# Routing's small operations moved ahead of a step's shares, masks behind them, and the low weight product last, in window attention followed by a top-1 mixture of experts

## Chip, cores and metric

The kernel runs on one core of one Trainium2 chip. The metric is the device time in microseconds (us) of one launch, the median of several runs.

## What is computed

Attention in a causal window of 64 positions (8 batches, 8 heads, 576 positions, 64 values a head), and behind it a mixture of 8 experts in which each of the 4608 tokens (rows of 512 values) goes to one expert only. The reference, cut:

```python
scores = scale * np.matmul(q, k.transpose(0, 1, 3, 2))
mask = (rel >= 0) & (rel < window)                 # window = 64
attn = softmax(np.where(mask, scores, -1e9))       # 1e-9 is added to the sum
x = np.matmul(attn, v)                             # to 4608 rows of 512
logits = x @ w_gate                                # 8 experts
expert_idx = np.argmax(logits, axis=1)
gate_w = softmax(logits)[np.arange(N), expert_idx]
for e in range(8):
    mask = expert_idx == e
    h = np.maximum(x[mask] @ w1[e], 0.0)           # 512 -> 1024
    out[mask] = gate_w[mask, None] * (h @ w2[e])   # 1024 -> 512
```

## The kernel before

All is written in the order in which each engine runs it; nothing reorders it later. Attention runs in 36 **steps** of 128 tokens (`NS`), counted by `i` in the loop at L797, and 7 more empty ones (`LAST`). It is a pipeline over steps: in step `i` the kernel makes the scores of tile `i`, the exponentials of tile `i-1`, the masks of `i-2`, the values and shares of `i-3`, the transposed rows of `i-4`. What one step issues on each engine:

- ScalarE (ACT): `exps(i-1)`, eight Exp of 64 columns; `evac(i-2)`, the copy `tsb` of the transposed exponentials out of PSUM tile `t_b`; `cols_t(i-4)`, the copy `xT`; a piece of weight rounding `whi`.
- GpSimd (POOL): `apart(i-2)`, two multiplications `pm` of `tsb` with masks, 512 columns each. These are the **masks**.
- VectorE (DVE): `folded(i)` and `largest(i)` on the scores in `s_b` (L386, L392, L394); `shares(i-3)` (L438, L440, L442), which reads `x_b`, divides, and writes the row `xrow`; then a read of the logits, `lgT` (L495) in one step and `lgs` (L479) in the next; a piece of the weights' low part `wlo` (L228).
- TensorE (PE): `scores(i)` into `s_b`, `values(i-3)` into `x_b`, a product for the logits (also in `x_b`), `rows_t(i-4)` (L449), `transp(i-1)` (L407). Within `x_b` the next writer waits for the last reader, so `values` of a step waits for the `lgT` or `lgs` of the step before.

**Routing** runs in three rounds, of 14, 12 and 10 tiles. When the logits of a round's last tile have been read, `route` queues eight pieces, s1 to s8, in `slow`. s1 to s3 find each token's expert (`lm`, `ld`, `eq`, `em`, `oh` on DVE). s4 is PE's: it counts ranks (L528, L530), ACT copies them (`rks`), at the head of a step. s5 to s7 turn ranks into places (`pos`, `base`, `se`, `pf`, `g` on DVE; `se`, `fl`, `mid` on POOL). s8 splits them (`lo`, `val`), and then one-hot rows `hot_row` (`put`, L577) and their products `here`, `said` (L588 to L595) follow from the queue `puts`. From these PE makes a table (L602), DVE reads it (L607 to L615), and POOL fetches token rows by index (L172). Round 0 is routed in steps 19 to 26, round 1 in steps 31 to 37, so that experts 0 to 3 can begin on their first tokens while attention still runs.

From step 29 (`TURN`) on, `forward` lays pieces of the first experts' work (the generator `expert`) between a step's parts, and `turn` transposes fetched rows: PE into `t_b` or `m_b`, ACT `xeh`, DVE `xel`. From step 29 on `s_b` has one buffer for scores, and `rows_t` shares `t_b` with `turn`.

Each f32 product of the experts is made of three matmuls of rounded parts: high by high, high weights by low tokens, low weights by high tokens. An expert pass has 8 groups `j`; each has a first product of 12 matmuls into `m_b` or `t_b` (L293), then `hh` (ACT) and `hl` (DVE), and a second product of three matmuls for each of 2 or 3 blocks (L257). `yield` in `expert` marks where `forward` may cut. ACT's `whi` and DVE's `wlo` for group `j+1` are made while group `j` runs.

Of the kernel before, what the change touches and what calls it, by code (L numbers as in the profile page):

```python
# [24 lines left out]
P = 128  # L25
# [15 lines left out]
NS = N // P  # L41


ROUNDS = [14, 12, 10]
# [18 lines left out]
RATE = (3, 2)  # L63
# [51 lines left out]
def window_attention_then_top1_moe(ctx: ExitStack, tc: tile.TileContext, qkv, wall, wg, cst, out):  # L115
    nc = tc.nc
# [157 lines left out]
    def expert(xt, idx, gates, wts, following=None):  # L274


        xh, xl = xt
        nu = len(idx)
        w = nu * P
        yp = None  # L280
        cur = wts.first
        for j in range(NJ):
            if j + 1 < NJ:
                nxt = wts.split()
            elif following is not None:
                following().first = following().split()
            hi, lo = cur
            hp = bank("hp")
            m = 0
            for kk in range(4):  # L290
                ks = slice(kk * P, (kk + 1) * P)
                for a, x in ((hi, xh), (hi, xl), (lo, xh)):
                    nc.tensor.matmul(hp[:, 0:w], lhsT=a[:, ks], rhs=x[:, kk, 0:w], start=(m == 0), stop=(m == 11))  # L293
                    m += 1
                if kk < 3:
                    yield
            hh = hw.tile([P, WIDE * P], F32R, name="hh")
            hl = hw.tile([P, WIDE * P], F32R, name="hl")
            nc.scalar.activation(out=hh[:, 0:w], in_=hp[:, 0:w], func=AF.Relu)  # L299
            nc.vector.scalar_tensor_tensor(out=hl[:, 0:w], in0=hp[:, 0:w], scalar=0.0, in1=hh[:, 0:w],  # L300
                                           op0=ALU.max, op1=ALU.subtract)
            yield
            yield from flush()
            if yp is None:
                yp = [bank("yp") for u in range(nu)]
            late.append(((hh, hl), yp, cur, j, (idx, gates) if j == NJ - 1 else None))
            cur = nxt
            yield j
# [45 lines left out]
    def begin_routing():  # L354
        nc.vector.tensor_copy(out=tri, in_=cc("tri"))
        nc.vector.tensor_copy(out=base, in_=cc("ebase"))
        nc.vector.tensor_copy(out=val[:, :, 0], in_=cc("tcol"))
        nc.vector.tensor_copy(out=rowb, in_=cc("row"))
# [128 lines left out]
    slow, puts, begin = deque(), deque(), deque()  # L487
# [9 lines left out]
    def route(nt, lgs, t0, rnd):  # L497
# [80 lines left out]
                                    in1=v["lo"][:, a:b].unsqueeze(2).to_broadcast([P, b - a, P]), op=ALU.is_equal)  # L578


        again = (None,) if rnd + 1 < len(ROUNDS) else ()
        slow.extend((f in (None, s4), f) for f in (s1, s2, s3, *again, s4, s5, s6, s7, s8))

    def parts(pool, want, nt, nm):

# [177 lines left out]
    def each(f, n):  # L763
        if 0 <= n < NS:
            f(n)
# [4 lines left out]
    def first_passes():  # L770
        for e in range(EARLY):
            ms = range(2 * e, 2 * e + 2)
            for j in expert(xe[e % 2], cols(eidx, ms), cols(egate, ms), ew[e],
# [6 lines left out]
                        keep["turned"] = True  # L780
                yield e, j

    early = first_passes()

    def forward(i, place):
# [10 lines left out]
    with tc.manual_schedule():  # L796
        for i in range(NS + LAST):  # L797
# [10 lines left out]

            rs_["step"] = i
            if slow and slow[0][0]:  # L810
                f = slow.popleft()[1]
                if f:
                    f()
            while begin and begin[0][0] <= i:
                begin.popleft()[1]()
            each(exps, i - 1)
            each(evac, i - 2)
            each(apart, i - 2)
            while exs:
                exs.popleft()()  # L820
            if i > TURN:
# [4 lines left out]
            each(largest, i)  # L826
            if i == 3:
                begin_routing()
            if TURN - 2 <= i < TURN:
                turn(xg[0], i - TURN + 2, xe[0], m_b)  # L830
            forward(i, 1)
# [4 lines left out]
            if quarters:  # L836
                o, w = quarters.popleft()
# [9 lines left out]
            if rs_["read"]:  # L847
                rs_["read"]()
                rs_["read"] = None
            for k in range(RATE[0] if i < NS else 4):  # L850
                if slow and not slow[0][0]:
                    slow.popleft()[1]()
            for k in range(RATE[1] if i < NS else 4):
                if puts and not slow:
                    puts.popleft()()
            while lows:
                lows.popleft()()
            if pieces:
# [95 lines left out]
```

## Time and profile before

| what | value |
|---|---|
| three runs | 670.57, 672.99, 674.42 us; median 672.99 |
| the profiled execution | 670.88 us, of which its span 669.1 us |
| busy share of the span | PE 93%, DVE 62%, ACT 54%, POOL 29% |
| mean granted PE clock | 0.989 of full speed |
| chain that ended last | PE 73%, DVE 11%, issue 6%, ACT 3%, POOL 3%, DMA 2% |

The profile is of one execution. An instruction's time runs from its start to its end, and what stands in brackets behind a row is how long its engine had been idle and what it waited for. PE's rows overlap, since matmuls are pipelined: starts are read, not ends. Attention alone runs until about 133 us, attention beside the first experts until about 205, and the experts from there on.

### The profile page before, as it was taken

How to read it: one execution, taken by the hardware profiler on the slowest of the kernel's cores; microseconds unless marked ns; L12 is line 12 of the kernel's file. 1: busy time of each engine (PE TensorE's matmuls, PEld its weight loads, DVE VectorE, ACT ScalarE, POOL GpSimd, SP SyncE). 2: the span in 40 equal slices, each digit the busy share in tenths (PEclk: the TensorE clock that was granted, in tenths of full speed). 3: DMA queues.
4: the chain of work that ended last, by engine and by line, in shares of the span. 5: the costliest groups of instructions: out<-in, count | busy, mean ns of one | idle time of the engine just before them, and what ended most of it. 6: DMA issues, size and time to landing. Idle time of an engine off the chain costs nothing.

```text
span 669.1 us, 17037 instructions
## 1 busy us (share of the span) xinstructions
PE 619.5 (93%) x7001; PEld 546.9 (82%) x7001; DVE 413.4 (62%) x762; ACT 359.8 (54%) x758; POOL 193.0 (29%) x168
## 2 busy tenths in 40 slices
PE   6799976888998799999999999999999999999995
PEld 5688865666787688889999999999999999899994
DVE  3777789856775985654444565565556565555651
ACT  4576665555544344454545555655555565555551
POOL 4566654733543015121111131312212131110011
PEclk9999997899999999999999999999999999999998
DMA  9988887864037346664455676576667656555620
GB/s 318 325 282 271 276 291 219 247 212 158 35 132 278 128 157 221 259 225 152 145 171 173 229 225 207 198 233 232 208 225 229 223 195 230 209 203 189 220 95 33
DMA packets 35110, 138.13 MB, mean 206 GB/s; under 512 B 4940, under 2 KB 6092, under 8 KB 25552
## 3 DMA queue, kind: packets, MB, share of 16 engines
q1 hardware_dynamic: 28624, 118.08, 52.3%
q0 software_dynamic: 6400, 18.88, 8.3%
q8 instruction: 57, 0.93, 0.6%
q14 instruction: 29, 0.24, 0.1%
HBM read 119.11 MB, written 19.92 MB: 208 GB/s over the span
## 4 chain that ended last, share of the span: by engine, by line
PE 73%; DVE 11%; issue 6%; ACT 3%; POOL 3%; DMA 2%; POOLq 0%; DVEq 0%; ACTq 0%
PE m_b L293 16%; PE x_b L257 14%; PE s_b L257 14%; PE t_b L293 13%; PE x_b L432 5%; PE s_b L375 3%; POOL pm L418 3%; PE s_b L183 2%; DVE wlo L228 2%; ACT pf L402 2%; PE t_b L407 1%; PE x_b L494 1%; DMA raw<-wall 1%; PE m_b L449 1%; DVE s_b L392 1%
## 5 line engine op out<-in xcount | busy, mean ns | idle before, releaser
L228 DVE TENSOR_TENSOR wlo<-raw,whi 128x1024 fp32r<-128x1024 f32 (+1 forms) x158 | 188.0, 1191 | 165.3 <-ACT whi L231 164.4
L231 ACT CAST whi<-raw 128x1024 fp32r<-128x1024 f32 (+1 forms) x147 | 148.9, 1014 | 100.3 <-PE s_b L257 50.7
L418 POOL TENSOR_TENSOR pm<-tsb,cs 128x512 f32<-128x512 f32 x72 | 91.8, 1295 | 85.2 <-ACT tsb L411 75.2
L265 POOL DMA_INDIRECT out<-ys,idx_sb x32 | 40.7, 1273 | 181.6 <-ACT ys L264 176.7
L172 POOL DMA_INDIRECT xg<-xs,idx_sb x32 | 33.4, 1043 | 155.8 <-PE s_b L183 138.4
L402 ACT ACTIVATE pf<-s_b,mxs 128x64 f32<-128x64 f32 x288 | 63.1, 337 | 14.9 <-PE s_b L375 6.7
L293 PE MATMUL t_b<-xh,whi 128*128 128x256 f32 (+1 forms) x240 | 70.3, 293 | 0.0
L293 PE MATMUL m_b<-xh,whi 128*128 128x256 f32 (+1 forms) x240 | 70.3, 293 | 0.0
L257 PE MATMUL s_b<-whi,hh 128*128 128x512 f32 x176 | 70.0, 398 | 0.0
L293 PE MATMUL m_b<-xl,whi 128*128 128x256 f32 (+1 forms) x240 | 69.6, 290 | 0.2 <-DVE xl L186 0.2
L257 PE MATMUL s_b<-whi,hl 128*128 128x512 f32 x176 | 69.0, 392 | 0.6 <-DVE hl L300 0.6
L293 PE MATMUL t_b<-xl,whi 128*128 128x256 f32 (+1 forms) x240 | 69.4, 289 | 0.0
L293 PE MATMUL m_b<-xh,wlo 128*128 128x256 f32 (+1 forms) x240 | 69.3, 289 | 0.0
L293 PE MATMUL t_b<-xh,wlo 128*128 128x256 f32 (+1 forms) x240 | 69.2, 289 | 0.0
L257 PE MATMUL s_b<-wlo,hh 128*128 128x512 f32 x176 | 69.1, 393 | 0.0
L299 ACT ACTIVATE hh<-m_b 128x256 fp32r<-128x256 f32 (+1 forms) x82 | 32.6, 398 | 58.1 <-PE m_b L293 58.0
L432 PE MATMUL x_b<-ring,pm 64*64 64x65 f32 x2176 | 46.8, 226 | 13.4 <-DVE lgs L479 4.2
L432 PEld LDWEIGHTS x_b<-ring,pm 64*64 64x64 f32 x2176 | 41.5, 138 | 18.9 <-issue 12.6
L257 PE MATMUL x_b<-wlo,hh 128*128 128x512 f32 x144 | 56.5, 392 | 0.0
L257 PE MATMUL x_b<-whi,hl 128*128 128x512 f32 x144 | 56.4, 392 | 0.0
L257 PE MATMUL x_b<-whi,hh 128*128 128x512 f32 x144 | 56.3, 391 | 0.0
L300 DVE SCALAR_TENSOR_TENSOR hl<-m_b,hh 128x256 fp32r<-128x256 f32 (+1 forms) x82 | 35.4, 431 | 22.1 <-ACT hh L299 22.0
(178 smaller groups left out, 1275.6 us busy)
## 6 DMA issues: line engine op xcount, KB each, us to landing
raw<-wall SPq DMA_DIRECT2D x74, 1024.0 KB, 5.2
ring<-qkv SPq DMA_DIRECT2D x66, 386.0 KB, 4.4
xs<-xrow SPq DMA_DIRECT2D x36, 256.0 KB, 3.2
raw<-wall SPq DMA_DIRECT2D x8, 256.0 KB, 5.0
ring<-qkv SPq DMA_DIRECT2D x4, 256.0 KB, 4.8
ring<-qkv SPq DMA_DIRECT2D x4, 130.0 KB, 4.9
ring<-qkv SPq DMA_DIRECT2D x1, 512.0 KB
xg<-xs,idx_sb POOLq DMA_INDIRECT x32, 4.1
```

What stands on the lines that cost most here:

```text
L172: nc.gpsimd.indirect_dma_start(out=t[:, u], out_offset=None, in_=xs[0:rows], in_offset=bass.IndirectOffsetOnAxis(ap=ix, axis=0), bounds_ch ...
L228: nc.vector.tensor_tensor(out=lo[:, s], in0=raw[:, s], in1=hi[:, s], op=ALU.subtract)
L231: nc.scalar.copy(out=hi[:, s], in_=raw[:, s])
L257: nc.tensor.matmul(y, lhsT=x[:, us], rhs=w[:, C:], start=(j == 0 and m == 0), stop=(j == NJ - 1 and m == 2))
L265: ins = nc.gpsimd.indirect_dma_start(out=out, out_offset=bass.IndirectOffsetOnAxis(ap=ix, axis=0), in_=ys, in_offset=None, bounds_check=N ...
L293: nc.tensor.matmul(hp[:, 0:w], lhsT=a[:, ks], rhs=x[:, kk, 0:w], start=(m == 0), stop=(m == 11))
L299: nc.scalar.activation(out=hh[:, 0:w], in_=hp[:, 0:w], func=AF.Relu)
L300: nc.vector.scalar_tensor_tensor(out=hl[:, 0:w], in0=hp[:, 0:w], scalar=0.0, in1=hh[:, 0:w], op0=ALU.max, op1=ALU.subtract)
L375: nc.tensor.matmul(sp[cols, a, g], lhsT=q_r[rows, r, g], rhs=k_r[rows, r - 1:r + 1, g], start=True, stop=True)
L402: nc.scalar.activation(out=pf[:, g, a], in_=sp[:, a, g, 0], func=AF.Exp, bias=mx[:, h:h + 1], scale=SCALE)
L418: nc.gpsimd.tensor_tensor(out=pm[i], in0=t.rearrange("p (g q) -> p g q", g=NG), op=ALU.mult, in1=cc("mask")[:, i * P:(i + 1) * P].unsqueez ...
L432: nc.tensor.matmul(x_b[cols, a, g * V1:(g + 1) * V1], lhsT=pm[i][rows, g, cols], rhs=v_r[rows, c % RING - i, g], start=(i == 0), stop=(i = ...
```

## The change

1. Pieces of routing were run at a step's end, behind `shares` and the read. Now the function `routing` runs them right behind `largest(i)`, ahead of `turn`, `values` and `shares`, for steps below 36.
2. `apart` (the masks on POOL) was called at a step's head; now it is called behind `routing`.
3. Rounds 0 and 1 had an empty entry ahead of s4, which held it back by one step; it is gone. Since s1 to s3 now run a step later than before, s4 to s8 and the `puts` stay in the steps in which they were.
4. The first expert product runs its eight matmuls of the high weights first and its four of the low weights last, cut by `yield` after 4, 8 and 10 matmuls (before: after 3, 6 and 9, the low part third in each group of three).

```diff
             hp = bank("hp")
-            m = 0
             for kk in range(4):
                 ks = slice(kk * P, (kk + 1) * P)
-                for a, x in ((hi, xh), (hi, xl), (lo, xh)):
-                    nc.tensor.matmul(hp[:, 0:w], lhsT=a[:, ks], rhs=x[:, kk, 0:w], start=(m == 0), stop=(m == 11))
-                    m += 1
-                if kk < 3:
+                for x in (xh, xl):
+                    nc.tensor.matmul(hp[:, 0:w], lhsT=hi[:, ks], rhs=x[:, kk, 0:w], start=(kk == 0 and x is xh), stop=False)
+                if kk & 1:
+                    yield
+            for kk in range(4):
+                nc.tensor.matmul(hp[:, 0:w], lhsT=lo[:, kk * P:(kk + 1) * P], rhs=xh[:, kk, 0:w], start=False,
+                                 stop=(kk == 3))
+                if kk == 1:
                     yield
...
-        again = (None,) if rnd + 1 < len(ROUNDS) else ()
-        slow.extend((f in (None, s4), f) for f in (s1, s2, s3, *again, s4, s5, s6, s7, s8))
+        slow.extend((f is s4, f) for f in (s1, s2, s3, s4, s5, s6, s7, s8))
...
+    def routing(a, b):
+        for k in range(a):
+            if slow and not slow[0][0]:
+                slow.popleft()[1]()
+        for k in range(b):
+            if puts and not slow:
+                puts.popleft()()
...
             each(evac, i - 2)
-            each(apart, i - 2)
...
             each(largest, i)
             if i == 3:
                 begin_routing()
+            if i < NS:
+                routing(*RATE)
+            each(apart, i - 2)
...
-            for k in range(RATE[0] if i < NS else 4):
-                if slow and not slow[0][0]:
-                    slow.popleft()[1]()
-            for k in range(RATE[1] if i < NS else 4):
-                if puts and not slow:
-                    puts.popleft()()
+            if i >= NS:
+                routing(4, 4)
```

On DVE, from the read at the end of step 19 into step 20 (round 0; `lm` to `oh` are s1 to s3; the three rows on `s_b_75` are `folded` and `largest` of step 20), before:

```order
L479 TENSOR_REDUCE lgs<-x_b 128x16
L508 TENSOR_REDUCE lm<-lgs 128x14
L511 TENSOR_TENSOR ld<-lgs,lm 128x112
L513 SCALAR_TENSOR_TENSOR eq<-ld,cs_82 128x112
L520 TENSOR_REDUCE em<-eq 128x14
L522 MEMSET oh 128x4
L523 TENSOR_TENSOR oh<-eq,em 128x112
L386 COPY_PREDICATED s_b_75<-fold,s_b_75 128x8x64
L392 TENSOR_REDUCE s_b_75<-s_b_75 128x8
L394 TENSOR_SCALAR mxs<-s_b_75 128x8
L438 TENSOR_SCALAR den<-x_b 128x8
```

and after:

```order
L482 TENSOR_REDUCE lgs<-x_b 128x16
L389 COPY_PREDICATED s_b_75<-fold,s_b_75 128x8x64
L395 TENSOR_REDUCE s_b_75<-s_b_75 128x8
L397 TENSOR_SCALAR mxs<-s_b_75 128x8
L511 TENSOR_REDUCE lm<-lgs 128x14
L514 TENSOR_TENSOR ld<-lgs,lm 128x112
L516 SCALAR_TENSOR_TENSOR eq<-ld,cs_82 128x112
L523 TENSOR_REDUCE em<-eq 128x14
L525 MEMSET oh 128x4
L526 TENSOR_TENSOR oh<-eq,em 128x112
L441 TENSOR_SCALAR den<-x_b 128x8
```

The six small instructions changed places with the step's work on its scores; both still stand ahead of `den`, the first of `shares`.

On POOL, around step 21 of round 0 (`se`, `fl`, `mid` are routing's; the first `pm` pair of the list before is the masks of step 21, the pair behind `mid` those of step 22), before:

```order
L418 TENSOR_TENSOR pm_1908<-tsb,cs_81 128x512
L418 TENSOR_TENSOR pm_1909<-tsb,cs_81 128x512
L547 TENSOR_SCALAR se<-se 128x14
L554 TENSOR_SCALAR fl<-pf_1986 128x14
L556 TENSOR_SCALAR mid<-fl 128x14
L418 TENSOR_TENSOR pm_2007<-tsb,cs_81 128x512
L418 TENSOR_TENSOR pm_2008<-tsb,cs_81 128x512
```

and after:

```order
L550 TENSOR_SCALAR se<-se 128x14
L557 TENSOR_SCALAR fl<-pf_1936 128x14
L559 TENSOR_SCALAR mid<-fl 128x14
L421 TENSOR_TENSOR pm_1943<-tsb,cs_81 128x512
L421 TENSOR_TENSOR pm_1944<-tsb,cs_81 128x512
L421 TENSOR_TENSOR pm_2037<-tsb,cs_81 128x512
L421 TENSOR_TENSOR pm_2038<-tsb,cs_81 128x512
```

The masks of step 21 now stand behind three operations that wait for DVE's s6 and s7 of the same step. In the other steps POOL's order is as it was, and its masks wait for nothing on DVE.

On DVE, step 34 of round 1 (`xel` is `turn`'s, `lo` to `hot_row` are s8 and two one-hot operations), before:

```order
L386 COPY_PREDICATED s_b_75<-fold,s_b_75 128x8x64
L392 TENSOR_REDUCE s_b_75<-s_b_75 128x8
L394 TENSOR_SCALAR mxs<-s_b_75 128x8
L186 TENSOR_TENSOR xel_109<-t_b,xeh_108 128x4x128
L438 TENSOR_SCALAR den<-x_b 128x8
L440 RECIPROCAL rs<-den 128x8
L442 TENSOR_TENSOR xrow<-x_b,rs 128x512
L495 COPY lgT<-x_b 128x256
L560 SCALAR_TENSOR_TENSOR lo<-mid,pf_3318 128x12
```

and after:

```order
L389 COPY_PREDICATED s_b_75<-fold,s_b_75 128x8x64
L395 TENSOR_REDUCE s_b_75<-s_b_75 128x8
L397 TENSOR_SCALAR mxs<-s_b_75 128x8
L563 SCALAR_TENSOR_TENSOR lo<-mid,pf_3246 128x12
L566 CAST val<-g 128x12
L567 TENSOR_TENSOR g_3369<-g,val 128x12
L568 CAST val<-g_3369 128x12
L569 TENSOR_TENSOR val<-g_3369,val 128x12
L580 TENSOR_TENSOR hot_row<-rowb,lo 128x512 x2
L186 TENSOR_TENSOR xel_109<-t_b,xeh_108 128x4x128
```

s8 and the one-hot rows moved from behind `lgT` to ahead of `xel`, for which `rows_t` waits on PE.

## Rows read from the trace of the kernel before

**Rows 1.** The view of busy time by stretch: from:to in us, its length, then busy us of PE, its weight loads, DVE, ACT, POOL (instructions), the granted PE clock, the DMA share and GB/s.

```profile
100.00:125.00 25.00, 16.92 (x448) 14.52 (x441) 22.86 (x53) 12.66 (x46) 13.27 (x11) 0.86 0.72 215
225.00:250.00 25.00, 21.35 (x128) 18.50 (x129) 22.74 (x52) 10.65 (x17) 3.05 (x2) 1.00 0.43 150
357.00:642.00 285.00, 285.00 (x1863) 258.51 (x1862) 165.79 (x218) 166.17 (x246) 53.38 (x44) 1.00 0.63 215
```

**Rows 2.** The timeline of DVE, steps 19 to 26 (round 0): start us, duration us, engine, line, operation, out<-in, and in brackets the idle time before it and its releaser.

```profile
83.71 0.68 DVE L511 TENSOR_TENSOR ld<-lgs,lm 128x112 f32<-128x112 f32 x1
87.81 0.41 DVE L495 COPY lgT<-x_b 128x256 f32<-128x256 f32 x1
92.75 1.31 DVE L536 TENSOR_TENSOR pos<-rks,base 128x112 f32<-128x112 f32 x1
94.55 0.27 DVE L546 TENSOR_TENSOR pos<-pos,oh 128x112 f32<-128x112 f32 x1
99.98 2.36 DVE L577 TENSOR_TENSOR hot_row<-rowb,lo 128x512 bf16<-128x512 bf16 x2
102.27 1.48 DVE L228 TENSOR_TENSOR wlo<-raw,whi 128x256 fp32r<-128x256 f32 x1
106.37 1.02 DVE L577 TENSOR_TENSOR hot_row<-rowb,lo 128x512 bf16<-128x512 bf16 x2
107.30 0.42 DVE L228 TENSOR_TENSOR wlo<-raw,whi 128x256 fp32r<-128x256 f32 x1
109.69 0.17 DVE L438 TENSOR_SCALAR den<-x_b 128x8 f32<-128x8 f32 x1 [0.43 <-PE x_b L494]
112.64 0.70 DVE L386 COPY_PREDICATED s_b<-fold,s_b 128x512 f32<-128x512 int32 x1 [0.53 <-PE s_b L375]
115.36 1.01 DVE L592 TENSOR_TENSOR said<-here,val 128x56 bf16<-128x56 bf16 x1
117.52 1.20 DVE L611 TENSOR_TENSOR ix<-ix,tt 128x4 f32<-128x4 f32 x1
```

**Rows 3.** The timeline of POOL over the same steps, same columns; a row of `pm` x2 is one step's masks.

```profile
85.34 2.51 POOL L418 TENSOR_TENSOR pm<-tsb,cs 128x512 f32<-128x512 f32 x2 [1.08 <-ACT tsb L411]
91.42 2.50 POOL L418 TENSOR_TENSOR pm<-tsb,cs 128x512 f32<-128x512 f32 x2 [3.57 <-ACT tsb L411]
95.71 0.30 POOL L556 TENSOR_SCALAR mid<-fl 128x14 f32<-128x14 f32 x1
100.28 3.19 POOL L418 TENSOR_TENSOR pm<-tsb,cs 128x512 f32<-128x512 f32 x2 [1.82 <-ACT tsb L411]
117.43 2.51 POOL L418 TENSOR_TENSOR pm<-tsb,cs 128x512 f32<-128x512 f32 x2 [1.14 <-ACT tsb L411]
```

**Rows 4.** The timeline of PE over the same steps, same columns.

```profile
82.88 1.10 PE L375 MATMUL s_b<-ring 64*64 64x128 f32 x32
88.28 0.21 PE L528 MATMUL x_b<-oh,tri 128*128 128x120 bf16 x1 [0.78 <-DVE lgT L495]
93.98 1.05 PE L432 MATMUL x_b<-ring,pm 64*64 64x65 f32 x56 [0.65 <-POOL pm L418]
99.39 1.16 PE L432 MATMUL x_b<-ring,pm 64*64 64x65 f32 x64 [1.74 <-DVE lgT L495]
106.59 2.01 PE L432 MATMUL x_b<-ring,pm 64*64 64x65 f32 x64 [3.76 <-DVE lgs L479]
116.57 0.50 PE L602 MATMUL x_b<-said,hot_row 128*128 128x20 bf16 x14 [1.83 <-DVE said L595]
```

**Rows 5.** The timelines of DVE, POOL and PE in steps 33 and 34 (round 1), same columns.

```profile
173.05 1.16 DVE L228 TENSOR_TENSOR wlo<-raw,whi 128x1024 fp32r<-128x1024 f32 x1
174.12 0.68 DVE L386 COPY_PREDICATED s_b<-fold,s_b 128x512 f32<-128x512 int32 x1
175.66 0.68 DVE L186 TENSOR_TENSOR xel<-t_b,xeh 128x512 fp32r<-128x512 f32 x1
165.63 2.51 POOL L418 TENSOR_TENSOR pm<-tsb,cs 128x512 f32<-128x512 f32 x2 [7.02 <-ACT tsb L411]
173.49 1.15 PE L432 MATMUL x_b<-ring,pm 64*64 64x65 f32 x48
176.39 0.66 PE L449 MATMUL t_b<-cs,xrow 128*128 128x128 f32 x4 [0.62 <-DVE xel L186]
```

**Rows 6.** The view of waits, PE, first 290 us: who waited for whom, us in total, times, the longest.

```profile
PE m_b L293 <- DVE wlo L228: 4.6, 8, 0.8
PE t_b L293 <- DVE wlo L228: 2.7, 2, 1.4
```

**Rows 7.** Two of these waits, in PE's timeline.

```profile
207.39 0.38 PE L293 MATMUL m_b<-xeh,wlo 128*128 128x256 f32 x1 [0.76 <-DVE wlo L228]
221.32 0.39 PE L293 MATMUL t_b<-xeh,wlo 128*128 128x256 f32 x1 [1.41 <-DVE wlo L228]
```

**Rows 8.** The chain of waits that ended last, in order of time, 196 to 292 us: start us, us, engine, tile, line, count.

```profile
233.46 0.38 PE m_b L293
...
247.14 1.45 PE m_b L293 x10
...
275.03 1.46 PE m_b L293 x10
...
281.13 1.43 PE m_b L293 x12
```

More of the change, by code (lines that the diff above doesn't have):

```diff
@@ L810, in window_attention_then_top1_moe @@
             if slow and slow[0][0]:
-                f = slow.popleft()[1]
-                if f:
-                    f()
+                slow.popleft()[1]()
             while begin and begin[0][0] <= i:
```

## The prediction, on record before the result

> **What bounds the kernel now.** I read the busy time by stretch first [rows 1]. From 357 to 642 us PE is busy for all of 285.00 us: nothing there can be won but by fewer matmuls, and there are as many after as before. So the change acts ahead of that, and what PE gains or loses by then moves the end by as much. Between 100 and 125 us PE works 16.92 of 25 us while DVE works 22.86, and the granted clock is 0.86: that is routing's round 0. Between 225 and 250 us DVE works 22.74 of 25: the experts' start, where DVE feeds PE.
>
> The timelines of round 0 come next. PE waits 1.74 us for `lgT` at 99.39, 3.76 for `lgs` at 106.59, 1.83 for `said` at 116.57 [rows 4]: DVE is late each time. Why it is late stands in its own rows [rows 2]: instructions with two inputs in SBUF last far longer when masks run beside them on POOL. `pos` took 1.31 us where the next such operation of the same 112 columns took 0.27; it ended at 94.06, just behind the masks of 91.42 to 93.92 [rows 2, 3]. Two `hot_row` took 2.36 at 99.98 and 1.02 at 106.37; a `wlo` piece 1.48 and 0.42; `ix`, four columns only, 1.20, from 117.52 until the first mask operation begun at 117.43 was over. One operation of masks lasts 1.25 (half of 2.50), and a DVE instruction that meets one waits it out; of two in a row each can wait for one.
>
> Last, PE's waits for `wlo` [rows 6]: ten, 4.6 + 2.7 = 7.3 us.
>
> **Part A, routing in round 0.** No instruction is added or removed, so I keep a ledger of DVE's lost time from the end of `lgs` in step 19 (about 83.4, 0.3 ahead of `ld`) to the end of `said`, for which the table at 116.57 waits. Left out is DVE's wait for the rank matmul and the scores behind it, the same either way. *Before* [rows 2]: `ld` 0.68 for 0.27, 0.41 lost; `pos` 1.04; hot rows and `wlo` piece 3.84 for 1.44, 2.40; waits for a PE at low clock 0.43 + 0.53; `said` 1.01 for 0.27 at most, 0.74. Sum 5.5 us.
>
> *After*, step by step. Step 20: the scores end at 82.88 + 1.10 [rows 4], so DVE, free at 83.4 and with no small operations left to fill the gap, idles 0.6 to 0.7. Copy, maximum and scaling (0.70 + 0.70 + 0.17 less overlaps, 1.6) bring it to 85.6, and there the masks have just begun, 85.34 to 87.85 [rows 3]. `ld` waits for the first, `eq` for the second: 1.9 lost. `lgT` so ends near 90.2, not 88.2, and the rank matmul, which waited for it at 88.28 [rows 4], comes 1.9 later, with ACT's `rks` and the exponentials queued behind. Step 21: `pos` and its like are free, since the masks now stand behind `mid` on POOL: 0 lost. But these masks, 91.42 before, wait for `mid`: `pos` issues at about 93.5 (90.2, then 1.7 for ranks and scores, 1.6 for copy and maximum), and `mid`, 95.71 + 0.30 before, came 3.3 behind `pos`, 2.2 without the 1.04 that it lost. So they begin near 95.6, and `values`, which had them at 93.98, at about 98.2; the masks of step 22 follow at once, 98 to 100.5. Into them fall step 21's `wlo` piece (0.4 lost), s8 (its first two-input operation waits one mask, the next the other: 1.5) and the following piece (0.7). Step 23 is free. In steps 24 and 25 `here`, `said` follow `largest` just when masks run (in step 20 these begin 1.4 us behind the end of the scores, and `largest` ends 1.6 behind it): 0.95 + 1.45. Sum 0.7 + 1.9 + 0.4 + 1.5 + 0.7 + 0.95 + 1.45 = 7.6. The difference is **+2.0 us**. Already in it: PE's 3.76 us gap goes, and with it the low clock behind (64 matmuls of `values` in 2.01 us at 106.59, in 1.16 at 99.39, where only 1.74 of idling lay ahead).
>
> Bounds: if DVE's instructions never met masks only 0.7 + 1.4 of this stays (idling, and one wait in s8 or a piece), −3.4; if they meet them as reckoned and PE, which now idles near 98, drops its clock there, +3.5. I take +2.0, nearest to the rows of `pos` and `ix`.
>
> The Trainium skill, page "SBUF — State Buffer", section "Who interferes with whom", says that a DVE instruction with two SBUF inputs contends with a GpSimd instruction that reads SBUF, and that the one issued second is fully blocked until the first is done; reductions and inputs from PSUM stay free. The 1.20 us of `ix` agree. It speaks against this change: by it the ledger after stands at 7.6, and without it at −3.4 against before.
>
> **Part A, round 1** [rows 5]. s1 to s3 move into a step in which DVE idles for the experts' `hh`: 0. In step 33 the masks (165.63 before) wait for s5 to s7 and end at about 172.4; `values` takes them at 173.49: hidden by 1 us, and if that cover went it would cost what is over. s5 to s7 (1.3) leave the road to the copy of step 34, but the `wlo` ahead of it (1.16, at 173.05) now meets these masks, so the copy comes at 173.5 for 174.12, −0.6. Then the loss: s8 (five small ones, 0.85 by the 0.17 of `den`) and two hot rows (1.02) stand ahead of `xel`, and the masks of step 34's tile, pushed to about 173.5 to 176, hold s8 up by 0.9. `xel` goes from 175.66 to 177.8. PE's `rows_t` already waited 0.62 for it at 176.39, in-order, with everything behind it: **+2.0 us**. Bounds: +1.2 without masks beside, and 0 if PE's next wait absorbs it; I see none large enough.
>
> POOL's fetches keep their place, and SP's queue does not change at all.
>
> **Part B, low product last.** The first low matmul stands ninth, not third. Twelve take 1.43 us [rows 8], 0.119 each, so it comes 6 × 0.119 = 0.71 later, and each wait for `wlo` shrinks by up to 0.71. All ten would give at most 5.7 (the shorter ones end at zero). But from about 216 to 233 us, and on to 247, the chain runs on DVE: there PE merely waits again at the next group. Gains count only where the chain steps from `wlo` to PE: 207.39 [rows 7], 233.46, 247.14 and 275.03 [rows 8], 4 × 0.71 = **−2.9 us**; 221.32, the longest wait, is not one. Bounds −0.7 (the last one only) and −5.7. It adds no matmul, and `hh` starts no later, as only four matmuls are left when `wlo` lands.
>
> **The sum.** 2.0 + 2.0 − 2.9 = +1.1 us. Against the profiled 670.88 (its span 669.1 and 1.8 around it) that is 672.0; that execution lay 2.1 below the median of 672.99, so for a median I forecast 672.99 + 1.1 = **674.1 us**.
>
> **Rivals.** *Routing pays* (chance 0.22): the small operations fall into DVE's waits for PE and miss the masks, because POOL runs later than I think. Then A is about −2 in round 0 and +1 in round 1, B −4 as DVE is freer: −5, 668.0. For it speak the 1.74 + 3.76 + 1.83 = 7.3 us that PE loses to DVE between 99 and 117 [rows 4]; against it, that masks begin within 0.3 us of the end of `largest`, as reckoned for step 20.
>
> *Slower, by the masks' new place* (0.20): in steps 21 and 33 masks wait for `mid`. PE then idles from about 95 to 98 with eight matmuls between. It decides from the point where PE's clock falls behind this gap, as it did behind 3.76 us of idling and did not behind 1.74 [rows 4]. `values` to `transp` at half rate cost 2 more, by the 0.85 us that the 64 matmuls of `values` alone lost at 106.59: A +3.8 and +2.2, B only −1.5: +4.5, 677.5.
>
> *The change does nothing* (0.08): DVE sets the pace whatever the order, B is worth its last wait only (−0.7), and round 1's `xel` is absorbed: 672.3.
>
> **Numbers.** My forecast has 0.50, with 671 to 677 as its own range. The measurement tells apart about 0.5%, 3.4 us: below 669.6 lies rival one but for its upper part, 0.20; above 676.4 rival two and the forecast's top, 0.27; between 0.53. The range 668 to 678 leaves out the far bounds of A and of B.
>
> **What would show it.** Right: the rank matmul of round 0 about 2 us later behind step 19's `lgs`; `ld`, `eq`, `lo`, `here` of 0.7 to 1.3 us beside a `pm`; masks right behind `mid`; no gap of 3.8 us ahead of `values`; a PE wait of about 2.7 for `xel` in step 34; no wait for `wlo` over 0.7 but at DVE's slowest. Wrong: small operations at 0.2 to 0.3 throughout, or a granted clock below 0.9 in two stretches of round 0.

## The result, and the profile after

The changed kernel takes 676.25 us by the median of 7 executions (673.91 to 679.3), the kernel before, run beside it, 672.99: a ratio of 1.0052 (95% interval 1.0029 to 1.0075). Run unedited twice more, each time beside the kernel before, it gave 1.0002 (0.9983 to 1.0020) and 1.0038 (1.0011 to 1.0064). The mean of the three is 1.0031, 2.1 us slower; the forecast was 1.1 us slower. The intervals of the first two do not overlap: this kernel's time differs from set to set by more than within one. The first profiled execution took 676.52 us with a span of 674.7; that of before had a span of 669.1.

The views are read in the order used before. First the busy time by stretch (columns as in [rows 1]):

```profile
100.00:125.00 25.00, 18.82 (x489) 15.96 (x487) 23.75 (x58) 14.42 (x54) 12.68 (x10) 0.90 0.77 238
225.00:250.00 25.00, 21.80 (x128) 18.05 (x129) 23.36 (x63) 11.31 (x18) 3.05 (x2) 1.00 0.48 167
360.00:645.00 285.00, 285.00 (x1857) 258.24 (x1856) 166.91 (x220) 164.66 (x244) 52.38 (x43) 1.00 0.63 214
```

From 360 us on PE is never idle, as in [rows 1], so the whole difference arises ahead of that. DVE is busier in both other stretches.

The timeline of DVE, steps 19 to 26 (columns as in [rows 2]; the helpers' line numbers are 3 higher than before):

```profile
82.54 0.21 DVE L482 TENSOR_REDUCE lgs<-x_b 128x16 f32<-128x64 f32 x1
...
85.34 0.77 DVE L514 TENSOR_TENSOR ld<-lgs,lm 128x112 f32<-128x112 f32 x1
86.14 1.23 DVE L516 SCALAR_TENSOR_TENSOR eq<-ld,cs 128x112 f32<-128x112 f32 x1
...
92.70 0.27 DVE L539 TENSOR_TENSOR pos<-rks,base 128x112 f32<-128x112 f32 x1
...
95.22 1.00 DVE L228 TENSOR_TENSOR wlo<-raw,whi 128x256 fp32r<-128x256 f32 x1
...
98.55 1.30 DVE L566 CAST val<-g 128x14 bf16<-128x14 f32 x1
...
104.84 2.11 DVE L580 TENSOR_TENSOR hot_row<-rowb,lo 128x512 bf16<-128x512 bf16 x2
...
109.92 0.98 DVE L590 TENSOR_TENSOR here<-mid,cs 128x56 bf16<-128x56 f32 x1
...
114.99 1.26 DVE L597 TENSOR_SCALAR said<-here,cs 128x56 bf16<-128x56 bf16 x1
...
117.21 0.22 DVE L482 TENSOR_REDUCE lgs<-x_b 128x16 f32<-128x64 f32 x1
```

POOL and then PE in the same steps (two fences, same columns):

```profile
84.72 2.53 POOL L421 TENSOR_TENSOR pm<-tsb,cs 128x512 f32<-128x512 f32 x2 [1.08 <-ACT tsb L414]
...
94.42 0.30 POOL L559 TENSOR_SCALAR mid<-fl 128x14 f32<-128x14 f32 x1
94.68 5.12 POOL L421 TENSOR_TENSOR pm<-tsb,cs 128x512 f32<-128x512 f32 x4
103.72 2.95 POOL L421 TENSOR_TENSOR pm<-tsb,cs 128x512 f32<-128x512 f32 x2 [3.92 <-ACT tsb L414]
108.30 2.52 POOL L421 TENSOR_TENSOR pm<-tsb,cs 128x512 f32<-128x512 f32 x2 [1.63 <-ACT tsb L414]
113.73 2.49 POOL L421 TENSOR_TENSOR pm<-tsb,cs 128x512 f32<-128x512 f32 x2 [2.90 <-ACT tsb L414]
```

```profile
89.41 0.21 PE L531 MATMUL x_b<-oh,tri 128*128 128x120 bf16 x1 [1.17 <-DVE lgT L498]
...
96.00 0.35 PE L435 MATMUL x_b<-ring,pm 64*64 64x65 f32 x8 [1.71 <-POOL pm L421]
97.40 1.13 PE L435 MATMUL x_b<-ring,pm 64*64 64x65 f32 x56 [1.06 <-POOL pm L421]
98.46 1.08 PE L497 MATMUL x_b<-xT,wg_sb 128*32 128x128 f32 x16
...
103.20 1.16 PE L435 MATMUL x_b<-ring,pm 64*64 64x65 f32 x64 [0.62 <-DVE lgT L498]
...
108.27 1.16 PE L435 MATMUL x_b<-ring,pm 64*64 64x65 f32 x64 [1.63 <-DVE lgs L482]
...
117.47 0.50 PE L604 MATMUL x_b<-said,hot_row 128*128 128x20 bf16 x14 [2.16 <-DVE lgs L482]
```

To be seen: what was long in [rows 2] (`pos` 1.31) is short, and other instructions are long in its place, each beside a row of `pm`. The rank matmul comes 6.87 us behind the start of step 19's `lgs`, 5.12 before (88.28 − 83.16). The masks stand right behind `mid`, and `values` waits for them twice. The gap of 3.76 in [rows 4] is gone, and with it the low clock behind it. But the clock is low in two other places: at 98 to 102 us, behind the two waits of `values`, it is 0.55 and 0.59 by stretches of 2 us (the product for the logits takes 1.08 us at 98.46, and 0.64 before), and behind the wait at 117.47 it is 0.50 (64 matmuls of `values` take 1.97 at 118.94). The table no longer waits for `said`, which ends at 116.25, but for `lgs` behind it: the moved rows reach it by pushing `shares` and the read back. From `lgs` to the table it is 117.47 − 82.54 = 34.93 us, before 116.57 − 83.16 = 33.41.

Round 1, steps 33 and 34 (DVE, POOL, PE; [rows 5] is the same place before):

```profile
174.20 1.22 DVE L228 TENSOR_TENSOR wlo<-raw,whi 128x1024 fp32r<-128x1024 f32 x1
175.63 0.69 DVE L389 COPY_PREDICATED s_b<-fold,s_b 128x512 f32<-128x512 int32 x1 [0.22 <-PE s_b L378]
...
177.18 0.62 DVE L563 SCALAR_TENSOR_TENSOR lo<-mid,pf 128x12 f32<-128x12 f32 x1
...
178.44 1.28 DVE L580 TENSOR_TENSOR hot_row<-rowb,lo 128x512 bf16<-128x512 bf16 x2
179.64 0.69 DVE L186 TENSOR_TENSOR xel<-t_b,xeh 128x512 fp32r<-128x512 f32 x1
171.26 2.54 POOL L421 TENSOR_TENSOR pm<-tsb,cs 128x512 f32<-128x512 f32 x2
180.38 1.12 PE L452 MATMUL t_b<-cs,xrow 128*128 128x128 f32 x4 [1.98 <-DVE xel L186]
```

`xel` starts 4.01 us behind the start of the copy, 1.54 before, and PE waits 1.98 us for it, 0.62 before; its four matmuls behind take 1.12 us for 0.66. As in step 21, the masks of step 33 now stand behind `mid`: in this round too POOL's order is another than before.

PE's waits for `wlo`, first 290 us (7.3 us before, [rows 6]):

```profile
PE t_b L296 <- DVE wlo L228: 1.8, 2, 1.1
PE m_b L296 <- DVE wlo L228: 0.3, 1, 0.3
```

And one place that nothing in the change explains. ScalarE's timeline and the busy time by stretch, 269 to 278 us:

```profile
269.53 1.04 ACT L231 CAST whi<-raw 128x1024 fp32r<-128x1024 f32 x1
274.07 0.38 ACT L302 ACTIVATE hh<-t_b 128x256 fp32r<-128x256 f32 x1 [3.50 <-PE m_b L296]
```

```profile
272.00:274.00 2.00, 0.62 (x4) 0.42 (x4) 0.00 (x0) 0.00 (x0) 0.70 (x1) 1.00 0.97 348
...
276.00:278.00 2.00, 2.00 (x11) 1.90 (x10) 2.00 (x3) 0.61 (x1) 0.00 (x0) 0.50 0.47 76
```

`t_b`, which `hh` reads, was complete at 269.5, yet ScalarE does nothing from 270.57 until 274.07; PE stands still behind it and then runs at 0.50 of its clock, 1.2 GHz.

### The profile page after: what moved, and what is told of

It reads as the page before. It is cut to its first block, busy times and chain, and to the rows that moved or that the text cites. A ratio compares the mean times of both kernels' runs of the same rounds, so it can differ in the third digit from the quotient of the medians.

```text
span 674.7 us, 17036 instructions
## 1 busy us (share of the span) xinstructions
PE 624.0 (92%) x7001; PEld 550.7 (82%) x7001; DVE 415.4 (62%) x762; ACT 359.3 (53%) x758; POOL 191.0 (28%) x168
## 4 chain that ended last, share of the span: by engine, by line
PE 74%; DVE 11%; issue 6%; POOL 4%; ACT 3%; DMA 2%; POOLq 0%; DVEq 0%; ACTq 0%
PE s_b L257 15%; PE x_b L257 14%; PE m_b L292 11%; PE t_b L292 9%; PE m_b L296 6%; PE t_b L296 5%; PE x_b L435 4%; PE s_b L378 3%; POOL pm L421 3%; PE s_b L183 2%; PE t_b L410 2%; DVE wlo L228 1%; ACT pf L405 1%; DVE s_b L395 1%; DVE s_b L389 1%
## 5 line engine op out<-in xcount | busy, mean ns | idle before, releaser
L292 PE MATMUL m_b<-xh,whi 128*128 128x256 f32 (+1 forms) x240 | 63.7, 294 | 0.0
L292 PE MATMUL t_b<-xh,whi 128*128 128x256 f32 (+1 forms) x240 | 63.6, 294 | 0.0
L292 PE MATMUL m_b<-xl,whi 128*128 128x256 f32 (+1 forms) x240 | 62.7, 290 | 0.2 <-DVE xl L186 0.2
L292 PE MATMUL t_b<-xl,whi 128*128 128x256 f32 (+1 forms) x240 | 62.4, 289 | 0.0
L302 ACT ACTIVATE hh<-t_b 128x256 fp32r<-128x256 f32 (+1 forms) x70 | 27.9, 399 | 41.7 <-PE t_b L296 35.7
L378 PE MATMUL s_b<-ring 64*64 64x128 f32 x1024 | 44.9, 300 | 2.8 <-ACT pf L405 2.5
```

The costliest lines, as they stand in the source:

```text
L292: nc.tensor.matmul(hp[:, 0:w], lhsT=hi[:, ks], rhs=x[:, kk, 0:w], start=(kk == 0 and x is xh), stop=False)
L378: nc.tensor.matmul(sp[cols, a, g], lhsT=q_r[rows, r, g], rhs=k_r[rows, r - 1:r + 1, g], start=True, stop=True)
```

## The experiments

The runs came in three sets, each beside the kernel before; the first two were on one chip, the third on another. The expectations are quoted from the record; the ratio is to the kernel before.

**The low product alone, twice.** The kernel before with this hunk of the diff only:

```diff
-                for a, x in ((hi, xh), (hi, xl), (lo, xh)):
-                    nc.tensor.matmul(hp[:, 0:w], lhsT=a[:, ks], rhs=x[:, kk, 0:w], start=(m == 0), stop=(m == 11))
...
+                for x in (xh, xl):
+                    nc.tensor.matmul(hp[:, 0:w], lhsT=hi[:, ks], rhs=x[:, kk, 0:w], start=(kk == 0 and x is xh), stop=False)
...
+            for kk in range(4):
+                nc.tensor.matmul(hp[:, 0:w], lhsT=lo[:, kk * P:(kk + 1) * P], rhs=xh[:, kk, 0:w], start=False,
+                                 stop=(kk == 3))
```

> The kernel before with the second part of the change alone: the first product's four low matmuls stand last; routing and masks as before. My theory of the result: this part gains what the prediction counted, about -2.9 us against before (bounds -0.7 and -5.7), most of it ahead of 285 us, and the waits of PE for wlo fall from 7.3 to about 2 us. Rival: the profile of after lost its gain again in a standstill at 270 to 276 us, because the later low matmuls let PE and DVE meet there; then this kernel shows the same standstill and gains 0.5 us or less, or loses.

> The kernel before with the low product last and nothing else, a second time, beside the others of this call. By the profiles so far the part is worth 3.0 to 3.5 us between 184 and 282 us; so -2.9 to -4 against before. If its first ratio (0.9922) is the better measure, -5. It should lie 3 to 5 us below the whole change.

Measured: 0.9922 (0.9893 to 0.9951) and 0.9955 (0.9927 to 0.9983), 5.2 and 3.0 us faster. The waits for `wlo` fall to 2.0 us. The part gains what was predicted or more: the second interval (−4.9 to −1.1 us) holds −2.9, the first (−7.2 to −3.3) lies beyond it. The second run lies 5.6 us below the whole change beside it, more than the 3 to 5 expected. Its profile shows a standstill of ScalarE (last section), and it gains all the same; the first profile has none.

**Routing's move alone.** The change without that hunk, so against it:

```diff
-                for x in (xh, xl):
...
+                for a, x in ((hi, xh), (hi, xl), (lo, xh)):
```

> The change with the first expert product as before: only routing's small operations, one-hot rows and masks are moved. My theory: this part costs more than the +4.0 of the prediction, +5 to +6.5 us against before: about +1.5 to 2 in round 0 (steps 19 to 26) and +3.5 to 4 in the round of steps 31 to 35. Rival: the move of the masks and rows is free or a gain and the loss measured for the whole change comes from the product's order; then -1 to +1.

Measured: 1.0072 (1.0042 to 1.0101), 4.8 us slower, just under my theory's 5 and far from the rival's −1 to +1. So the two parts pull against each other: 4.8 − 4.1 (the mean of the two above) = 0.7 us lies between what the three runs of the whole change cost.

**Round 0 and the product, without round 1.**

```diff
             each(evac, i - 2)
+            if i >= TURN:
+                each(apart, i - 2)
...
-            if i < NS:
+            if i < TURN:
                 routing(*RATE)
-            each(apart, i - 2)
+                each(apart, i - 2)
...
-            if i >= NS:
-                routing(4, 4)
+            if i >= TURN:
+                routing(*(RATE if i < NS else (4, 4)))
```

(With it the empty entry of the queue, `again`, is back for round 1 alone.)

> The change, but from step 29 on routing, rows and masks stand where they stood before; so round 0 and the low product are changed, the round of steps 31 to 35 is not. My theory: the difference from the whole change is that round, 3.5 to 4 us, so this is -1 to -0.3 us against before (round 0 +2, low product -2.9). Rival: round 0 is the loss and the later round costs only the +2.0 that was predicted; then +1 to +2.

Measured: 0.9961 (0.9938 to 0.9984), 2.6 us faster; the first theory's side, and more than its 0.3 to 1. So undoing round 1 alone turns the loss into a gain.

**Masks back at the head.**

```diff
             each(evac, i - 2)
+            each(apart, i - 2)
...
             if i < NS:
                 routing(*RATE)
-            each(apart, i - 2)
```

> The change with one edit undone: the masks stand at the head of a step as before, while the small operations and the rows keep their new place. If the masks' new place (behind mid on GpSimd, so that values and scores wait) is what makes the change slow, this is 2 to 4 us faster than the whole change, about 0 against before. If the masks' place is hidden, as the prediction had it for the later round, and the cost is the rows and small operations ahead of xel, this is within 1 us of the whole change, about +3. A third outcome, slower than the whole change, would say that masks at the head meet the small operations more often.

Measured: 1.0004 (0.9977 to 1.0031). Against the whole change's mean of 1.0031 that is 1.8 us less; against its second run (1.0002), on the same chip and without a standstill as here, it is the same. Its stages (table below) show that it is no clean answer: round 0 is longer by 3 us, round 1 shorter by 1.7.

**Rows at the step's end.**

```diff
-                routing(*RATE)
+                routing(RATE[0], 0)
...
                 rs_["read"] = None
+            if i < NS:
+                routing(0, RATE[1])
```

> The whole change, but the one-hot rows (hot_row, and here and said of the first experts' table) stay at a step's end as before; the small operations and the masks keep the new place. In the round of steps 31 to 35 two hot_row (1.2 us) leave the road to xel, five small operations stay on it: PE's wait for xel in step 34 falls from 2.4 to about 1.2 us and its clock holds behind it. In round 0 here and said no longer follow largest into the masks, but stand at the step's end, where they met them in the kernel before too: 0 to -1.5. So 2 to 3.5 us faster than the whole change run beside it. Rival: the small operations alone (s8 beside the masks) keep xel late; then within 1 us of the whole change.

Measured: 0.9992 (0.9966 to 1.0018), against 1.0038 for the whole change beside it: 3.1 us faster, as my theory had it; part of it lies in the experts (95.90 us against 98.25 in the table below), which this edit leaves alone. PE and then DVE of this kernel:

```profile
116.71 0.50 PE L604 MATMUL x_b<-said,hot_row 128*128 128x20 bf16 x14 [1.65 <-DVE said L597]
...
177.12 0.66 PE L452 MATMUL t_b<-cs,xrow 128*128 128x128 f32 x4 [1.23 <-DVE xel L186]
```

```profile
83.30 0.21 DVE L482 TENSOR_REDUCE lgs<-x_b 128x16 f32<-128x64 f32 x1
...
112.43 0.21 DVE L590 TENSOR_TENSOR here<-mid,cs 128x56 bf16<-128x56 f32 x1
...
116.42 0.23 DVE L597 TENSOR_SCALAR said<-here,cs 128x56 bf16<-128x56 bf16 x1
```

`here` takes 0.21 for 0.98, the last `said` 0.23 for 1.26; from `lgs` to the table it is 116.71 − 83.30 = 33.41 us, exactly before's. PE's wait for `xel` is 1.23, and its matmuls behind run in 0.66: the clock held.

**Routing behind `xel`**, first for the whole change, then with round 0 as before.

```diff
+            if TURN - 2 <= i < TURN:
+                turn(xg[0], i - TURN + 2, xe[0], m_b)
+            forward(i, 1)
             if i < NS:
                 routing(*RATE)
             each(apart, i - 2)
-            if TURN - 2 <= i < TURN:
-                turn(xg[0], i - TURN + 2, xe[0], m_b)
-            forward(i, 1)
             each(values, i - 3)
```

> The change with one move: from step 29 on the small operations, the rows and the masks stand behind the part of the experts that makes xel, and before values. If the rows and small operations ahead of xel are what costs in step 34, as the prediction said, this is 1.5 to 2.5 us faster than the whole change run beside it, and xel of step 34 is no later against its step than before. If the loss of that round is the masks' wait for mid (they are now later still), it is the same or up to 1.5 us slower.

Measured: 0.9940 (0.9917 to 0.9963), 4.2 us faster than the whole change beside it (1.0002), more than the 1.5 to 2.5 expected. `xel` of step 34 on DVE now follows `largest` at once:

```profile
176.91 0.17 DVE L397 TENSOR_SCALAR mxs<-s_b 128x8 f32<-128x8 f32 x1
176.99 0.68 DVE L186 TENSOR_TENSOR xel<-t_b,xeh 128x512 fp32r<-128x512 f32 x1
```

The masks are still behind `mid` here, and round 1 is as short as in the kernel before: in this round their place costs nothing by itself. The second kernel, against the whole change (with it the empty entry of the queue is back for round 0 alone):

```diff
             each(evac, i - 2)
+            if i < TURN:
+                each(apart, i - 2)
...
-            if i < NS:
-                routing(*RATE)
-            each(apart, i - 2)
...
             forward(i, 1)
+            if TURN <= i < NS:
+                routing(*RATE)
+            if i >= TURN:
+                each(apart, i - 2)
...
+            if i < TURN:
+                routing(*RATE)
             if i >= NS:
```

> Round 0 as in the kernel before; from step 29 on the small operations, rows and masks in the middle of a step, but behind the part of the experts that makes xel; low product last. My theory: with xel ahead of them the moved instructions cost and bring nothing in that round, so this is within 1 us of the low product alone (about -4 against before). Rival: used as filler for VectorE's waits they gain there; then 1 to 2 us faster than the low product alone, and this is the best version.

Measured: 0.9952 (0.9919 to 0.9984), beside 0.9955 for the low product alone: nothing gained, nothing lost, as far as intervals of 2 us either way can tell. As filler for DVE's waits in round 1 the small operations bring nothing that shows.

**Round 0 without its masks**, in the kernel before and in the changed one.

```diff
         t = tss.pop(n)
+        if 17 <= n <= 24:
+            pms[n] = keep["pm16"]
+            return
...
```

> The kernel before, leaving out the masks of tiles 17 to 24 (steps 19 to 26); their values are made with tile 16's masks instead, so routing sees other numbers there, and only the stretch up to the table at about 117 us is compared. If VectorE's long two-input instructions of round 0 come from GpSimd's masks beside them, ld, pos, the wlo pieces and hot_row fall to 0.27, 0.27, 0.42 and 1.02 us, and the stretch from step 19's lgs to the table, 33.4 us before, shrinks by 3 to 5 us. If they are long for another reason, they stay as long.

> The same edit in the changed kernel (masks of tiles 17 to 24 left out, tile 16's used instead). By my theory the masks cost this kernel 5 us or more in round 0 (ld, eq, s8's operations and said each waited for one, and values waits for masks behind mid), so the stretch from step 19's lgs to the table, 34.9 us after, falls to 29 to 30 us, no longer than the kernel before without them. Rival: the changed order itself costs (VectorE idle with nothing to fill its wait for the scores); then it stays 1.5 us or more above the kernel before without masks.

The changed kernel without these masks, DVE and then PE, and below it PE of the kernel before without them:

```profile
81.55 0.21 DVE L487 TENSOR_REDUCE lgs<-x_b 128x16 f32<-128x64 f32 x1
...
84.02 0.28 DVE L519 TENSOR_TENSOR ld<-lgs,lm 128x112 f32<-128x112 f32 x1
84.33 0.28 DVE L521 SCALAR_TENSOR_TENSOR eq<-ld,cs 128x112 f32<-128x112 f32 x1
```

```profile
111.08 0.50 PE L609 MATMUL x_b<-said,hot_row 128*128 128x20 bf16 x14 [0.91 <-DVE lgs L487]
```

```profile
113.82 0.50 PE L607 MATMUL x_b<-said,hot_row 128*128 128x20 bf16 x14 [1.55 <-DVE said L600]
```

From `lgs` to the table: after 111.08 − 81.55 = 29.53 us, before (its `lgs` at 83.00) 30.82. With the masks they were 34.93 and 33.41. So the masks cost the changed kernel 5.4 us there, the kernel before 2.6 (a little under the 3 to 5 expected), and without them the changed order is the faster by 1.3 us. These are single executions; with the masks, this stretch takes 33.0 to 34.0 us in the four kernels with round 0 as before and 34.4 to 36.2 in the six with it changed. The 5.4 and 2.6 hold `values`' own waits for masks as well as the lengthened instructions. Routing sees other numbers in these two, so their whole times aren't compared.

**The changed kernel again, twice.**

> The changed kernel once more, unedited, on the chip and beside the run of before that the other kernels of this call have. The profile of its first run has all engines standing still for 2.4 us at 270 to 276 us, with ScalarE waiting 3.50 us ahead of an hh whose input was ready. If this standstill belongs to the change, it is there again and the ratio is near 1.006. If it was one execution's bad luck, it is gone, the profiled span is about 672 and the low product's gain shows in full (xel of the third expert pass about +3.0 us behind before instead of +5.45).

> The changed kernel unedited, a third time. It came out 0.5% behind before at first and level with it the second time; the second profile lacks the standstill at 270 us that the first had. If the standstill goes with single executions, the ratio lies between the two, 1.000 to 1.004, and the profile shows it or not by chance. If it goes with the chip or the placement of a session, the ratio is at one of the two ends, 1.005 with a standstill or 1.000 without.

Measured: 1.0002 and 1.0038, intervals above. The second profile has no standstill at 270 us and its ratio is the low end. The third has it, and its ratio fits either expectation (1.000 to 1.004 by chance, or near 1.005 with a standstill):

```profile
274.90 0.39 ACT L302 ACTIVATE hh<-t_b 128x256 fp32r<-128x256 f32 x1 [3.52 <-PE m_b L296]
```

**All profiles by stage.** Four marks from DVE's timeline, in us: the start of `mxs` in step 19 and in step 31, the end of the fourth `xel` (step 35), the end of the ninth (named `xl`). The lengths are their differences: round 0, round 1, and the early experts, where the low product acts.

| kernel | four marks | round 0 | round 1 | experts |
|---|---|---|---|---|
| before | 82.00, 152.66, 184.61, 282.48 | 70.66 | 31.95 | 97.87 |
| low product alone | 83.28, 153.91, 187.07, 281.94 | 70.63 | 33.16 | 94.87 |
| the same again | 81.81, 152.71, 184.43, 281.10 | 70.90 | 31.72 | 96.67 * |
| behind `xel`, round 0 as before | 81.50, 152.37, 183.69, 279.94 | 70.87 | 31.32 | 96.25 * |
| changed | 81.37, 153.85, 189.76, 287.93 | 72.48 | 35.91 | 98.17 * |
| changed, second | 83.03, 154.63, 189.55, 284.52 | 71.60 | 34.92 | 94.97 |
| changed, third | 82.49, 156.72, 190.52, 288.77 | 74.23 | 33.80 | 98.25 * |
| routing's move alone | 81.35, 153.33, 188.83, 286.13 | 71.98 | 35.50 | 97.30 |
| without round 1's | 81.90, 155.14, 186.88, 281.21 | 73.24 | 31.74 | 94.33 |
| routing behind `xel` | 81.32, 155.03, 186.36, 281.03 | 73.71 | 31.33 | 94.67 |
| masks at the head | 80.69, 156.50, 189.80, 284.36 | 75.81 | 33.30 | 94.56 |
| rows at the end | 82.14, 152.85, 185.35, 281.25 | 70.71 | 32.50 | 95.90 * |

A star marks a profile with ScalarE's standstill ahead of `hh` (2.11 to 3.52 us). Round 0 as before: mean of four 70.8; changed: mean of six (the four with the change whole or alone and the two that leave round 0 so) 72.9. Round 1 as before (before, both of the low product alone, without round 1's) 32.1; changed (the three profiles of the changed kernel and routing's move alone) 35.0. Experts with the old product 97.6, with the new and no standstill 94.7.

## Why the prediction was right, and what it mis-sized

The time fell in the forecast's own range, and by its mechanism: two rounds of routing slower, the experts faster, a small loss left. By stage it reads +2.1, +2.9 and −2.9 us; the prediction had +2.0, +2.0, −2.9. That the stages add up to 2.1 us, as the mean of the three ratios does, is chance: the experts' −2.9 leaves out the profiles with a standstill, and the mean has one in two of its three. Of the 3.3 us by which the first median exceeds before's, about 3 are, by its profile, the standstill, which the forecast knew nothing of; without it (the second run) the change comes out at 0.1 us, −1.1 to +1.3. The stages are single executions: round 0 of the changed kernel alone spans 71.60 to 74.23.

**Round 0, +2.0 predicted, +2.1 measured.** The ledger held in most of its lines. `ld` and `eq` wait for one mask operation each: 0.50 + 0.95 us lost against the 0.27 and 0.28 that they take without masks, 1.9 predicted. The rank matmul is 1.75 late, about 2 predicted. `pos` is free; the masks stand behind `mid`, from 94.68, near 95.6 predicted; the `wlo` piece loses 0.6; s8 meets one mask operation, and it is the cast to `val` (1.30 for 0.18), not the first two-input operation. `here` and `said` meet them in steps 24 and 25, 0.77 + 0.29 + 1.03 lost where 0.95 + 1.45 was predicted. Two lines were wrong, and they offset each other. "Step 23 is free": its two `hot_row` took 2.11 for 1.02, beside the masks from 103.72. And the piece behind s8, put at 0.7, lost nothing (0.41 at 102.97). With DVE's wait of 0.74 for the scores the losses add up to 0.74 + 1.45 + 0.59 + 1.12 + 1.09 + 0.77 + 0.29 + 1.03 = 7.1 us, 7.6 predicted. A cost that the ledger did not have shows in two other kernels with round 0 changed (without round 1's, and routing behind `xel`): PE's clock falls at 90 to 93 us, and DVE waits 2.42 and 2.68 us for the scores of step 21 instead of 1.47. The experiment with the rows at the end shows that rows, `here` and `said` carry the round's net cost: with them back, 33.41 us again, although `ld` and `eq` stay long. That the losses at the front are paid back by `pos` and by the gap of 3.76 that goes is read from the rows and not tested.

That masks are the cause is shown by the two kernels without them: −5.4 and −2.6 us. The Trainium skill, page "SBUF — State Buffer", section "Who interferes with whom", has it that a DVE instruction with two SBUF inputs contends with a GpSimd instruction that reads SBUF, that copies, casts and scalar operations can contend with GpSimd too, in the modes in which they use two ports, and that the one issued second is fully blocked. `eq` (two inputs), the cast at 98.55 and the scalar `said` at 114.99 all took 1.2 to 1.3 us, about the length of a mask operation: by their lengths the trace agrees with both halves of the rule; in which mode an instruction ran it does not tell. The ledger had applied only the first half to s8.

**Round 1, +2.0 predicted, +2.9 measured: the term that was too small.** The step to `xel` was right, in size too: small operations and rows stand on the road, and PE's in-order wait passes it on. From `mxs` of step 31 to the start of `xel` of step 34 it takes 22.8 to 24.2 us in the four profiles with round 1 as before (mean 23.2) and 24.7 to 25.8 in the four with it changed (25.1): +1.9. In the second profile `xel` starts 2.87 us behind `mxs`, 0.09 before, where the prediction's 0.85 + 1.02 + 0.9 make 2.77; s8's `lo` (0.95 for 0.17) and `wlo` (1.67 for 1.16) meet masks as counted. What was missing is PE's clock, for which the sum had nothing in this round. PE of the changed kernel, second run, with its stretches, and then the third run:

```profile
180.11 0.66 PE L452 MATMUL t_b<-cs,xrow 128*128 128x128 f32 x4 [2.43 <-DVE xel L186]
...
182.86 0.63 PE L257 MATMUL s_b<-whi,hh 128*128 128x512 f32 x1
```

```profile
180.00:182.00 2.00, 1.89 (x12) 1.89 (x13) 1.93 (x6) 1.19 (x5) 0.00 (x0) 0.74 0.02 7
182.00:184.00 2.00, 2.00 (x8) 1.53 (x7) 0.56 (x1) 2.00 (x8) 0.40 (x1) 0.50 0.32 124
```

```profile
182.21 0.65 PE L452 MATMUL t_b<-cs,xrow 128*128 128x128 f32 x4 [2.44 <-DVE xel L186]
...
184.27 0.40 PE L257 MATMUL s_b<-whi,hh 128*128 128x512 f32 x1
```

In both runs the wait is 1.8 over before's 0.62 and comes at full clock. In the second the granted clock is then 0.50 (1.2 GHz) from about 181 to 184 us, and a matmul of the second product takes 0.63 us; in the third, behind the same wait, the clock stays at 1.00 and it takes 0.40. From the start of this `xel` to the end of the next it is 10.18 us with the drop and 9.05 without, 8.95 before: 1.1 us, the clock's price, read from two runs of one kernel. The first run (10.13) and routing's move alone (10.50) have the drop too, so the mean of the four is 1.0 over before, which is what the term lacks. The length of this wait does not settle whether the clock falls: it fell behind 1.98, 2.43 and 2.62, and held behind 2.44, behind 1.98 with the masks at the head and behind 1.23 with the rows at the end. That the masks are hidden in step 33 held: with routing and masks behind `xel` the round takes 31.33 us.

**The low product, −2.9 predicted, −2.9 measured** where nothing stood still. The places agree in part. In the kernel with this product alone the shift against before moves by −1.04 us at 206 to 210, −0.28 at 236 to 240, −0.7 from 247 to 256 and −0.57 at 269 to 271 (counted were 207, 233, 247 and 275, at 0.71 each), and by −0.3 between 189 and 201, which was not counted. At 233, which was counted, it does not move. At 221, the longest wait, it gains nothing, as argued.

**What was not foreseen.** The standstill of ScalarE takes the experts' gain back in the first and third profile of the changed kernel: 98.2 us for 95.0, 3.2 us, about the 2.4 to 3.4 us by which these two ratios lie above the second. One execution of each was profiled, so that the others of these runs have it too is inferred.

**The rivals.** "Routing pays" would have come true without the masks: then the changed order is 1.3 us faster in round 0. It needed POOL to run later than reckoned, and POOL did not. "Slower, by the masks' new place" had its condition: in all three profiles of the changed kernel the clock falls behind the gap ahead of `values` (98 to 102 us in the first), and again behind the table, so that the sign of being wrong which the prediction named, a granted clock below 0.9 in two stretches of round 0, was there. Its price was not: from 98 us to the table no wait of DVE for PE shows in these profiles, and routing's move alone, whose clock is 1.00 from 60 to 125 us, takes 34.41 us from `lgs` to the table, 0.5 to 0.8 less than the three. PE's low clock there falls where DVE is the late one. "Does nothing" falls by the kernels with one part each, −5.2 and −3.0 against +4.8. The best kernels are those without the move of routing: the low product alone (0.9922, 0.9955); putting routing behind `xel` in round 1 adds nothing to it. The whole change with routing behind `xel` (0.9940) lies within their intervals, though its round 0 is 2.9 us longer; why that does not show in its time is open.

## What to carry to other kernels

Before small VectorE work is moved into a gap, look at what GpSimd does in that gap: here operations of 0.2 us that met a GpSimd instruction of 1.25 us took up to 1.3. Ask of each place which result behind it another engine waits for in order (here `xel`), and put the filler behind that, not ahead. Putting the operand that is made last at the end of a product's sum costs no instruction and shortened the waits for it here from 7.3 to 2.1 us, but counts only where the chain passes through that wait.

## What the runs showed of the hardware that was not expected

ScalarE can stand still for 2.11 to 3.52 us ahead of an instruction whose input is ready. Five of the twelve profiles in the table have it, always at the same `hh`, the second instruction behind two `ys` that start at 263 to 269 us; the rows of two stand above. In the changed kernel the DMA engines are then 0.95 to 0.97 busy, but the second profile, without a standstill, has 0.91 to 1.00 between 264 and 274 us as well.

It goes with the set of runs, so with the chip or the moment, more than with the kernel: all four profiles of the last set have it, none of the eight of the two sets before (the two without masks among them), and the first one of the changed kernel has it. No profile with the old order of the product (before, routing's move alone, before without masks) shows it, but none was taken in the last set, so whether that order would be spared is open. The DMA view shows one packet of the instruction queue within the 3 us ahead of it or in its first microsecond; it passes near there in all kernels, with or without standstill. That ScalarE waits for its instructions there is a guess that no run tested.
